# A three-block kernel on one core: float64 weights converted in the expert block and the last block, and the last block run as two passes over the tokens

## The chip, the cores and the metric

One core of a Trainium2 chip runs the program; the seven others are idle. The metric is the device time of one execution in microseconds, from the first to the last instruction with what lies around them; lower is better. The kernel before was timed three times: median 955.05 us, from 953.25 to 957.42.

## The reference

Three blocks follow each other. The second and third work on N = 4·576 = 2304 tokens of width 512.

```python
# 1 attention, B=4, H=8, S=576, D=64; bias is a small net of |i-j|, per head
scores = 0.125 * q @ k.T + bias[h]          # softmax over keys, then @ v
# 2 experts: E=8, each token goes to one expert, 512 -> 1024 -> 512
h  = np.maximum(x[mask] @ w1[e], 0.0);  out[mask] = gate * eom * (h @ w2[e])
# 3 last block, 512 -> 2048 -> 512; w_in and w_out are float64
h = x @ w_in;  g = h * np.cos(h);  out = g @ w_out
```

## The kernel before, in words

The program is one straight list of instructions, written in the order of the Python loops; every engine runs its own in that order and waits on semaphores. There are four stages.

**Bias table** (0 to 47.5 us): a table of biases is made and stored to DRAM.

**Attention** (47.5 to 305.7 us): 16 pairs of heads (`n`), each in five units `u` of two 128-row query tiles (the fifth has one). In a step, TensorE does the scores of unit `u` (L524, into two PSUM buffers `ps_s`), transposes the exponentials of the unit before (L560, into `Tp`), and does some of the products with V (L602; the table `AV_AT` says which of the ten products `(g, k)` stands how many steps after which unit). VectorE adds the bias and takes the row minimum (L534, which frees `ps_s`) and copies half of the transposes (L573); ScalarE does the exponentials (L545) and the other half (L571).

**Expert block** (`moe_dense`, 305.7 to 537.9 us): 64 steps of 24 matmuls, each float32 operand split into a high and a low part in the format fp32r, three products for one. L802 makes the low part of a weight tile on VectorE.

**Last block** (`moe2`, 537.9 us to the end): six groups of 384 tokens; for each, 16 chunks `f` of 128 hidden units; so 96 steps of 12 matmuls for the first layer (L1381, into `ph`) and 9 for the second (L1421, into three accumulators `py`), which runs four steps behind (`LAG3`). Between them the cosine: ScalarE L1316, VectorE L1321 to L1323, ScalarE L1395 and L1396, VectorE L1400, and then the split of `g` into `gh` (ScalarE L1406) and `gl` (GpSimd L1407). A group's sums leave through `o` (L1428 ScalarE, L1430 VectorE).

**The conversion.** `w_in` and `w_out` arrive as pairs of 32-bit words. The class `Doubles` cuts them into 64 pieces of 128 x 256 numbers. Each piece is loaded (L700, `raw`), turned into float32 by four VectorE instructions (L711 and L713 are a first `half()`, L716 and L718 a second) and an addition on GpSimd (L720), and stored to a DRAM tile `Wi` or `Wo` (L721), from where the last block's weights are loaded again (L792, `xc` or `Bp`), and split (L800, L802). `attention` converts 24 pieces: in each of pairs 1 to 12 a half after units 1 and 3 and two halves after unit 4 (`CV_AT`). `moe_dense` converts the other 40, as many halves in a step as a running cost on VectorE leaves room for (`STEP`, 3.2 us), the last ones behind its last step.

The order around the change is that of the Python calls. Two things in it matter. In attention, `softmax(n, u)` and, for `u` of 4, `convert(n, u)` follow each other, so that VectorE has the conversion ahead of the next pair's first L534. At the end of `moe_dense`, the remaining halves stand ahead of the last additions to `xT` (L1187) and of the last weight splits (L802), and the first tile `tk` of the last block (L1316) takes memory that the last of these splits reads.

Of the kernel before, what the change touches and what calls it, by code (L numbers as in the profile page):

```python
# [11 lines left out]
I32 = mybir.dt.int32  # L12
# [48 lines left out]
def build(tc, h, dbl, dbg=None):  # L61
    nc = tc.nc
    rw = dict(reuse_waits="tile")
    with ExitStack() as outer, ExitStack() as ctx:
# [17 lines left out]
            Wo=dpool.tile([DFF // 128, 128, DM], F32, name="Wo"),  # L82
        )
# [7 lines left out]
        with ExitStack() as low:  # L91
# [8 lines left out]
            attention(tc, h, ident, dram, xT, bpool, ps_t, gate, later, dense, cv)  # L100
# [17 lines left out]
        moe2(tc, h, dram, dense, later, wi, wo, magic)  # L118
# [283 lines left out]
def attention(tc, h, ident, dram, xT, bpool, ps_t, gate, later, dense, cv):  # L402
# [3 lines left out]
    with ExitStack() as ctx:  # L406
# [4 lines left out]
        cvp = low.enter_context(tc.tile_pool(name="p1d", bufs=2, side="right"))  # L411
# [66 lines left out]
        def after(G):  # L478
# [12 lines left out]
            if at == len(ROWS) - 1:  # L491
                load_v(1)
                gate.fetch()
                if cv:
                    cv.open(cvp, 24, 2, 3)
# [57 lines left out]
        def transposes(n, u):  # L553
# [8 lines left out]
            if u < 4:  # L562
# [52 lines left out]
        def convert(n, u):  # L615
            for _ in range(CV_AT[u] if cv and 0 < n < 13 else 0):
                cv.half()

# [4 lines left out]
        while t <= len(seq) or av:  # L623
            n, u = seq[t] if t < len(seq) else (None, None)
            if n is not None:
# [24 lines left out]
                if u == 4:  # L650
                    convert(n, u)
# [15 lines left out]
            if n is not None:  # L667
                if u < 4:
                    convert(n, u)
# [8 lines left out]
CV_AT = (0, 1, 0, 1, 2)  # L678
AV_AT = {1: ((0, 0, 1), (0, 1, 2), (0, 2, 2), (0, 3, 3)),
# [200 lines left out]
def moe_dense(tc, h, ident, dram, xT, dense, gate, later, cv):  # L880
    nc = tc.nc
    rw = dict(reuse_waits="tile")
    with ExitStack() as c2:
# [3 lines left out]
        if cv:  # L887
            cv.open(dpool, 40, 3, 2)
# [31 lines left out]
        for s in range(len(seq) + LAG2):  # L920
# [26 lines left out]
            if s in (NEXT_AT, NEXT_AT + 1):  # L947
                dense.load(B, s - NEXT_AT, 4, True)
# [18 lines left out]
X_AT, X2_AT, ADD_AT, GROUP_AT, HALF_AT, NEXT_AT = 21, 34, 48, 57, 60, 61  # L967
# [239 lines left out]
def doubles(tc, h, dram):  # L1207

    pieces = []
    for half in range(2):  # L1210
        for q in range(4 * half, 4 * half + 4):
            for c in range(NP_):
                pieces.append((h["w_in"].bitcast(I32)[128 * c:128 * c + 128, 512 * q:512 * q + 512], dram["Wi"][q, :, c, :]))
    for c in range(DFF // 128):
        for i in range(2):
            pieces.append((h["w_out"].bitcast(I32)[128 * c:128 * c + 128, 512 * i:512 * i + 512],
                           dram["Wo"][c, :, 256 * i:256 * i + 256]))
# [117 lines left out]
def moe2(tc, h, dram, dense, later, wi, wo, bias):  # L1335
# [4 lines left out]
    with ExitStack() as ctx:  # L1340
        pool = lambda name, bufs, **kw: ctx.enter_context(tc.tile_pool(name=name, bufs=bufs, reuse_waits="tile", **kw))
        xp, wp, gp, tp, op = (pool("p3x", 1), pool("p3w", 1), pool("p3g", 5), pool("p3t", 3), pool("p3o", 3))
        ps_h, ps_o = pool("ps_h", 5, space=PSUM), pool("ps_y", 1, space=PSUM)
        xg, xsp, d = {}, {0: dense.group}, {}
# [29 lines left out]
        def layer1(s):  # L1374
            g, f = divmod(s, FC)
# [35 lines left out]

        def layer2(s):
            g, f = divmod(s, FC)
            hi, lo = d[s]["hi"], d[s]["lo"]
            del d[s]
            if f == 0:
                acc[:] = [ps_o.tile([128, DM], F32, name=f"py{t}") for t in range(GT // 128)]
            for t in range(GT // 128):
                ts_ = slice(128 * t, 128 * t + 128)
                for n, (x, w) in enumerate(((hi, w_out[f][0]), (hi, w_out[f][1]), (lo, w_out[f][0]))):  # L1420
                    nc.tensor.matmul(acc[t], x[:, ts_], w, start=(f == 0 and n == 0), stop=(f == FC - 1 and n == 2))  # L1421
                if f == FC - 1:
                    o = op.tile([128, DM], F32, name="o")
                    out = h["out"][g * GT + 128 * t:g * GT + 128 * t + 128, :]
                    final = s == G * FC - 1 and t == GT // 128 - 1
                    near, far = (slice(0, DM // 2), slice(DM // 2, DM)) if final else (slice(0, DM),) * 2
                    if t % 2 == 0:
                        nc.scalar.activation(out=o[:, near], in_=acc[t][:, near], func=AF.Copy, scale=-2.0)  # L1428
                    if t % 2 or final:
                        nc.vector.tensor_scalar(out=o[:, far], in0=acc[t][:, far], scalar1=-2.0, scalar2=None,  # L1430
# [94 lines left out]
```

## Time and profile before

| | |
|---|---|
| three runs, median | 955.05 us |
| the profiled execution | 953.91 us, span 952.1 us, mean granted clock 0.987 |
| TensorE matmul busy | 917.5 us (96%) |
| VectorE busy | 651.8 us (68%) |
| ScalarE busy | 541.1 us (57%) |
| GpSimd busy | 303.5 us (32%) |

The profile is one execution; a line such as L524 is a line of the kernel before. Matmuls are pipelined and each row has its latency in it, so that TensorE counts as busy also where short bubbles lie between groups of matmuls. What a group really takes is the distance from its start to the next group's start. PE is TensorE, PEld its weight loads, DVE is VectorE, ACT ScalarE, POOL GpSimd, and SPq the queue of SyncE, which issues nearly all DMAs.

### The profile page before, as it was taken

The numbers are of one execution on the slowest core, as the hardware profiler recorded it, in microseconds if no ns is written. First come the engines' busy times: TensorE is split into PE (matmuls) and PEld (weight loads), VectorE is DVE, ScalarE is ACT, GpSimd is POOL, SyncE is SP. The second block draws the span as 40 slices with busy tenths as digits, with TensorE's granted clock in tenths as the row PEclk, the third lists the DMA queues.
The fourth block names the chain that finished last, engine by engine and source line by source line (L and its number), as shares of the span: only waits on it lengthen the run. The fifth ranks groups of instructions, "written<-read, shape, count | busy, mean of one in ns | idle before, by whom it ended". The sixth has DMA issues, their size and how long they took to land.

```text
span 952.1 us, 19180 instructions
## 1 busy us (share of the span) xinstructions
PE 917.5 (96%) x7145; PEld 779.4 (82%) x7146; DVE 651.8 (68%) x1472; ACT 541.1 (57%) x1153; POOL 303.5 (32%) x406
## 2 busy tenths in 40 slices
PE   7989999999999999999999989999999999999997
PEld 4666666666666899999899979999999999999995
DVE  8948888888867677788699898354444544544542
ACT  7967777777777434253263476455544554554542
POOL 0034554545555021213231225223233232232222
PEclk9979999999999999999999999999999999999999
DMA  7883536644537473537868531010100200100001
GB/s 215 275 293 111 170 123 218 199 146 139 183 115 243 155 244 135 181 100 232 276 224 277 193 115 52 1 67 1 50 17 1 67 1 1 67 1 1 34 1 36
DMA packets 62241, 118.04 MB, mean 124 GB/s; under 512 B 6664, under 2 KB 21532, under 8 KB 62140
## 3 DMA queue, kind: packets, MB, share of 16 engines
q1 hardware_dynamic: 61708, 116.45, 37.6%
q8 instruction: 58, 0.95, 0.4%
q14 instruction: 43, 0.35, 0.1%
q10 hardware_dynamic: 432, 0.29, 0.1%
HBM read 83.11 MB, written 33.60 MB: 123 GB/s over the span
## 4 chain that ended last, share of the span: by engine, by line
PE 69%; DVE 5%; DMA 2%; ACT 2%; issue 1%; POOL 0%; SPq 0%; DVEq 0%; POOLq 0%; ACTq 0%
PE py L1421 21%; PE ph L1381 20%; PE pl L854 9%; PE po L872 8%; PE pa L602 3%; PE ps_s L524 3%; PE Tp L560 2%; DMA Wo<-f32a 1%; DVE f32a L713 1%; ACT e L545 1%; DVE w1l L802 1%; DVE f32a L711 1%; DVE s L534 1%; DMA Fd<-lp 1%; DVE xl L826 0%
## 5 line engine op out<-in xcount | busy, mean ns | idle before, releaser
L1407 POOL TENSOR_TENSOR gl<-tg,gh 128x384 fp32r<-128x384 f32 x96 | 97.8, 1020 | 277.3 <-ACT gh L1406 163.6
L1316 ACT ACTIVATE tk<-ph,magic 128x384 f32<-128x384 f32 x96 | 55.5, 580 | 165.8 <-PE ph L1381 165.8
L1321 DVE TENSOR_SCALAR tk<-tk 128x384 f32<-128x384 f32 x96 | 36.6, 381 | 156.5 <-ACT tk L1316 156.5
L1381 PE MATMUL ph<-xh,w0l 128*128 128x384 f32 x384 | 129.5, 337 | 0.0
L1381 PE MATMUL ph<-xl,w0h 128*128 128x384 f32 x384 | 129.2, 336 | 0.0
L1381 PE MATMUL ph<-xh,w0h 128*128 128x384 f32 x384 | 129.2, 336 | 0.0
L1421 PE MATMUL py<-w1h,gh 128*128 128x512 f32 x288 | 113.7, 395 | 4.1 <-ACT gh L1406 4.1
L545 ACT ACTIVATE e<-s,mn 128x576 f32<-128x576 f32 x144 | 110.2, 767 | 6.5 <-DVE mn L534 6.3
L1421 PE MATMUL py<-w1h,gl 128*128 128x512 f32 x288 | 113.8, 395 | 0.0
L1421 PE MATMUL py<-w1l,gh 128*128 128x512 f32 x288 | 113.3, 393 | 0.0
L720 POOL TENSOR_TENSOR f32a<-f32a,raw 128x256 f32<-128x256 f32 x64 | 49.2, 769 | 195.9 <-DVE raw L718 174.0
L534 DVE CUSTOM_DVE_ANT_0 s<-ps_s,Bp 128x576 f32<-128x576 f32 x112 | 81.0, 755 | 40.8 <-PE ps_s L524 32.4
L524 PEld LDWEIGHTS ps_s<-HL 64*128 64x128 f32 x768 | 58.1, 191 | 38.6 <-DVE mn L534 20.0
L524 PE MATMUL ps_s<-HL 64*128 64x288 f32 x768 | 77.5, 319 | 10.3 <-DVE mn L534 8.8
L857 ACT ACTIVATE hh<-pl 128x288 fp32r<-128x288 f32 x64 | 26.3, 410 | 101.1 <-PE pl L854 98.0
L854 PE MATMUL pl<-xh,w0h 128*128 128x288 f32 x256 | 78.3, 306 | 1.8 <-DVE hl L858 1.8
L602 PE MATMUL pa<-eT,V 128*64 128x320 f32 (+1 forms) x512 | 79.4, 420 | 0.0
L854 PE MATMUL pl<-xl,w0h 128*128 128x288 f32 x256 | 76.4, 299 | 2.4 <-DVE xl L826 2.4
L854 PE MATMUL pl<-xh,w0l 128*128 128x288 f32 x256 | 75.5, 295 | 0.0
L872 PE MATMUL po<-hh,w1h 128*128 128x288 f32 x256 | 75.5, 295 | 0.0
L872 PE MATMUL po<-hl,w1h 128*128 128x288 f32 x256 | 75.5, 295 | 0.0
L872 PE MATMUL po<-hh,w1l 128*128 128x288 f32 x256 | 75.4, 295 | 0.0
(226 smaller groups left out, 2222.1 us busy)
## 6 DMA issues: line engine op xcount, KB each, us to landing
Bp<-in_w SPq DMA_DIRECT2D x38, 512.0 KB, 5.3
Bd<-ev SPq DMA_DIRECT2D x36, 295.5 KB, 4.7
Rqk<-in_qk SPq DMA_DIRECT2D x16, 576.0 KB, 5.6
raw<-in_w_in SPq DMA_DIRECT2D x32, 256.0 KB, 4.4
raw<-in_w_out SPq DMA_DIRECT2D x32, 256.0 KB, 3.8
Bp<-Bd SPq DMA_DIRECT2D x28, 288.0 KB, 5.1
X<-xT SPq DMA_DIRECT2D x7, 1152.0 KB, 5.6
V<-in_v SPq DMA_DIRECT2D x16, 320.0 KB, 4.2
```

Of the source, the lines that this page charges most:

```text
L524: nc.tensor.matmul(p[:, hf, :HF], w, y, start=(x == 0), stop=(x == 2))
L534: nc.vector.tensor_tensor_reduce(out=h2(s), in0=ps[:, :, :HF], in1=h2(bias(hp, i)), scale=-0.125, scalar=3e38, op0=ALU.add, op1=ALU.min, a ...
L545: nc.scalar.activation(out=e[:, par, :], in_=s, func=AF.Exp, bias=mn, scale=-1.0, accum_out=acc)
L602: nc.tensor.matmul(pa[64 * par:64 * par + 64, :W], d["V"][:, k, par, :], x, start=(k == 0), stop=(k == 4))
L720: self.tc.nc.gpsimd.tensor_tensor(out=af[:], in0=af[:], in1=low, op=ALU.add)
L854: nc.tensor.matmul(ps[:, :HF], w[:, c, :], x[:, c, :], start=(n == 0), stop=(n == len(terms) - 1))
L872: nc.tensor.matmul(self.acc[d][:, :HF], w[:, ds_], x, start=(f == 0 and n == 0), stop=(f == self.FC - 1 and n == 2))
L1316: nc.scalar.activation(out=k, in_=hh, func=AF.Identity, scale=INV2PI, bias=magic)
L1321: nc.vector.tensor_scalar(out=k, in0=k, scalar1=-MAGIC, scalar2=None, op0=ALU.add)
L1381: nc.tensor.matmul(ps[:, :GT], w[:, c, :], x[:, c, :], start=(n == 0), stop=(n == 3 * NP_ - 1))
L1407: nc.gpsimd.tensor_tensor(out=lo, in0=g, in1=hi.bitcast(F32), op=ALU.subtract)
L1421: nc.tensor.matmul(acc[t], x[:, ts_], w, start=(f == 0 and n == 0), stop=(f == FC - 1 and n == 2))
```

## The change

Conversion leaves attention altogether. The expert block converts 32 pieces (the first halves of `w_in` and of `w_out`), the last block the other 32, one or two halves in a step from its second step on. So that the second half of the weights is wanted later, the last block runs over the tokens twice: groups 0 to 5 with hidden chunks 0 to 7, whose sums are stored to a DRAM tile `Y1`, and then groups 5 to 0 with chunks 8 to 15, which add them back. Tokens of five groups are loaded and split a second time. Loads of the late weights stand at steps 13, 24, 34 and 45 (`LATE_AT`). In attention the products with V move: of the four of the first query half that came one, two, two and three steps after their unit, two now come at two steps and two at three; and the second copy of unit 3's transposes moves from ScalarE to VectorE. A constructor argument (`dynamic_dma_scratch_size=1024`) makes room in SBUF.

```diff
@@ attention
-            if at == len(ROWS) - 1:  ...  cv.open(cvp, 24, 2, 3)
-                    if qh == 0 or u == 3:
+                    if qh == 0:
                         nc.scalar.activation(out=dst, in_=Tp[qh], func=AF.Copy)
-                if u == 4:
-                    convert(n, u)
...
-CV_AT = (0, 1, 0, 1, 2)
-AV_AT = {1: ((0, 0, 1), (0, 1, 2), (0, 2, 2), (0, 3, 3)),
+AV_AT = {1: ((0, 0, 2), (0, 1, 2), (0, 2, 3), (0, 3, 3)),
@@ moe_dense
-            cv.open(dpool, 40, 3, 2)
+            cv.open(dpool, 32, 3, 2)
-            if s in (NEXT_AT, NEXT_AT + 1):
-                dense.load(B, s - NEXT_AT, 4, True)
@@ doubles: first half of w_in, first half of w_out, then quarter by quarter
+    for which in range(2):
+        for q in range(4):
+            part(which, q)
+    for q in range(4, 8):
+        for which in range(2):
+            part(which, q)
@@ moe2
+        HC = FC // 2
+        units = [(g, 0) for g in range(G)] + [(g % G, 1) for g in range(G - 1, 2 * G - 1)]
+        at = lambda s: (*units[s // HC], s % HC)
...
-                if f == FC - 1:
+                if j == HC - 1:
                     o = op.tile([128, DM], F32, name="o")
...
+                    if half == 0:
+                        if t % 2 == 0:
+                            nc.scalar.activation(out=o, in_=acc[t], func=AF.Copy, scale=-2.0)
+                        else:
+                            nc.vector.tensor_scalar(out=o, in0=acc[t], scalar1=-2.0, scalar2=None, op0=ALU.mult)
+                        nc.sync.dma_start(out=dram["Y1"][rows(g, t), :], in_=o)
+                        continue
+                    final = s == len(units) * HC - 1 and t == GT // 128 - 1
+                    for c in (slice(0, DM // 2), slice(DM // 2, DM)) if final else (slice(0, DM),):
+                        nc.vector.scalar_tensor_tensor(out=o[:, c], in0=acc[t][:, c], scalar=-2.0, in1=y1[t][:, c],
+                                                       op0=ALU.mult, op1=ALU.add)
...
+        if cv:
+            cv.open(cp, 32, 3, 2)
+        for q, when in zip(range(4, 8), LATE_AT):
...
+            if cv and s:
+                for _ in range(1 + s % 2):
+                    cv.half()
...
+                if nx != g:
+                    if j == 0:
+                        load_x(nx)
...
+                if half and j == 2:
+                    load_y(g)
+LATE_AT = (13, 24, 34, 45)
```

VectorE in attention, from the last L534 of unit 3 to the first of the next pair (`s` and `mn` are the biased scores and their minimum, `eT` the transposes' copy). Before:

```order
L534 ISA s,mn<-ps_s,Bq 128x576
L534 ISA mn 128x1
L573 COPY eT_930<-Tp 128x2x4x64
L716 TENSOR_SCALAR raw_1633<-f32a 128x256
L718 SCALAR_TENSOR_TENSOR raw_1633<-raw_1633 128x256
L534 ISA s,mn<-ps_s,Bq 128x576
L534 ISA mn 128x1
L711 TENSOR_SCALAR f32a<-raw_1656 128x256
L713 SCALAR_TENSOR_TENSOR f32a<-raw_1656,f32a 128x256
L716 TENSOR_SCALAR raw_1656<-f32a 128x256
L718 SCALAR_TENSOR_TENSOR raw_1656<-raw_1656 128x256
L534 ISA s,mn<-ps_s,Bp 128x576
```

Now (L532 is the former L534, L571 the former L573):

```order
L532 ISA s,mn<-ps_s,Bq 128x576
L532 ISA mn 128x1
L571 COPY eT_924<-Tp 128x2x4x64
L532 ISA s,mn<-ps_s,Bq 128x576
L532 ISA mn 128x1
L571 COPY eT_924<-Tp 128x2x4x64
L532 ISA s,mn<-ps_s,Bp 128x576
```

Six conversion instructions are gone from ahead of the last two L534 there, and one copy has come.

TensorE in the same place, from the scores of unit 3 to those of the next pair's second unit. Before:

```order
L524 MATMUL ps_s<-HL 128x288 x12
L560 MATMUL Tp<-ident,e 128x64 x16
L602 MATMUL pa_927<-eT_929,V 64x256 x2
L524 MATMUL ps_s<-HL,QR_126 128x288 x6
L560 MATMUL Tp<-ident,e 128x64 x16
L602 MATMUL pa_927<-eT_929,V 64x256 x4
L592 MATMUL Tp<-ident,et 128x128 x4
L524 MATMUL ps_s<-HL 128x288 x12
L560 MATMUL Tp<-ident,e 128x64 x10
L602 MATMUL pa_927<-eT_929,V 64x256 x2
L524 MATMUL ps_s<-HL 128x288 x12
```

Now:

```order
L522 MATMUL ps_s<-HL 128x288 x12
L558 MATMUL Tp<-ident,e 128x64 x16
L522 MATMUL ps_s<-HL,QR_126 128x288 x6
L558 MATMUL Tp<-ident,e 128x64 x16
L600 MATMUL pa_921<-eT_923,V 64x256 x4
L590 MATMUL Tp<-ident,et 128x128 x4
L522 MATMUL ps_s<-HL 128x288 x12
L558 MATMUL Tp<-ident,e 128x64 x10
L600 MATMUL pa_921<-eT_923,V 64x256 x4
L522 MATMUL ps_s<-HL 128x288 x12
```

Two matmuls with V have gone from unit 3's step to the next pair's first step.

VectorE at the turn from the expert block to the last block (L1187 adds to `xT`, L802 is a weight's low part, L711 to L718 the conversion, L1321 to L1323 the reduction of the first angles). Before:

```order
L711 TENSOR_SCALAR f32a<-raw_8302 128x256
L713 SCALAR_TENSOR_TENSOR f32a<-raw_8302,f32a 128x256
L716 TENSOR_SCALAR raw_8302<-f32a 128x256
L718 SCALAR_TENSOR_TENSOR raw_8302<-raw_8302 128x256
L1187 SCALAR_TENSOR_TENSOR xT<-xb,ohb,xT 128x288 x2
L1187 SCALAR_TENSOR_TENSOR xT<-xa,ohb,xT 128x288 x2
L802 TENSOR_TENSOR w1l_5432<-Bp,w1h_5431 128x1024
L802 TENSOR_TENSOR w1l_5434<-Bp,w1h_5433 128x1024
L1321 TENSOR_SCALAR tk<-tk 128x384
L1322 SCALAR_TENSOR_TENSOR tr<-tk,ph 128x384
L1323 SCALAR_TENSOR_TENSOR tr<-tk,tr 128x384
```

Now (L1175 is the former L1187, L792 the former L802, L701 to L708 the conversion, L1318 to L1320 the reduction):

```order
L1175 SCALAR_TENSOR_TENSOR xT<-xb,ohb,xT 128x288 x2
L1175 SCALAR_TENSOR_TENSOR xT<-xa,ohb,xT 128x288 x2
L792 TENSOR_TENSOR w1l_5213<-Bp,w1h_5212 128x1024
L792 TENSOR_TENSOR w1l_5215<-Bp,w1h_5214 128x1024
L1318 TENSOR_SCALAR tk<-tk 128x384
L1319 SCALAR_TENSOR_TENSOR tr<-tk,ph 128x384
L1320 SCALAR_TENSOR_TENSOR tr<-tk,tr 128x384
L701 TENSOR_SCALAR f32a<-raw_8190 128x256
L703 SCALAR_TENSOR_TENSOR f32a<-raw_8190,f32a 128x256
L706 TENSOR_SCALAR raw_8190<-f32a 128x256
L708 SCALAR_TENSOR_TENSOR raw_8190<-raw_8190 128x256
```

The last two of the conversion's pieces stood ahead of the additions to `xT` before (one is shown); now none does, and a whole piece follows the first reduction.

## Rows read from the trace of the kernel before

**Rows 1.** Busy time by stretch: turn to the last block, last block; us, engines, PEclk, DMA.
```profile
537.90:556.50 18.60, 14.49 (x73) 13.07 (x72) 16.33 (x29) 11.39 (x20) 3.67 (x5) 0.91 0.19 59
556.50:944.70 388.20, 388.20 (x1948) 351.63 (x1946) 203.55 (x384) 199.22 (x408) 118.61 (x115) 1.00 0.09 29
```
**Rows 2.** Chain that ended last, in order of time: start us, us, what.
```profile
552.74 3.90 PE py L1421 x9
...
650.76 2.10 PE py L1421 x9
```
**Rows 3.** Page part 5, groups: busy us, mean ns, then idle before and releaser.
```profile
L1421 PE MATMUL py<-w1h,gh 128*128 128x512 f32 x288 | 113.7, 395 | 4.1 <-ACT gh L1406 4.1
...
L720 POOL TENSOR_TENSOR f32a<-f32a,raw 128x256 f32<-128x256 f32 x64 | 49.2, 769 | 195.9 <-DVE raw L718 174.0
...
L854 PE MATMUL pl<-xh,w0h 128*128 128x288 f32 x256 | 78.3, 306 | 1.8 <-DVE hl L858 1.8
```
**Rows 4.** Timeline of VectorE at the turn to the last block.
```profile
537.67 0.85 DVE L711 TENSOR_SCALAR f32a<-raw 128x256 int32<-128x256 int32 x1
...
541.97 1.43 DVE L1187 SCALAR_TENSOR_TENSOR xT<-xb,ohb,xT 128x288 f32<-128x288 f32 x2
...
544.18 2.35 DVE L802 TENSOR_TENSOR w1l<-Bp,w1h 128x1024 fp32r<-128x1024 f32 x2
```
**Rows 5.** Timeline of ScalarE at the turn to the last block.
```profile
546.62 1.06 ACT L1316 ACTIVATE tk<-ph,magic 128x384 f32<-128x384 f32 x2 [5.51 <-PE ph L1381]
...
552.18 0.51 ACT L1406 ACTIVATE gh<-tg 128x384 fp32r<-128x384 f32 x1
```
**Rows 6.** Timeline of TensorE, 171 to 176 us: a pair's turn with a conversion.
```profile
172.35 1.07 PE L524 MATMUL ps_s<-HL 64*128 64x288 f32 x12
...
175.34 0.94 PE L524 MATMUL ps_s<-HL 64*128 64x288 f32 x10 [0.28 <-DVE mn L534]
```
**Rows 7.** Timeline of VectorE in the same stretch, 171 to 176 us.
```profile
171.11 1.08 DVE L711 TENSOR_SCALAR f32a<-raw 128x256 int32<-128x256 int32 x1
...
173.85 0.75 DVE L534 CUSTOM_DVE_ANT_0 s<-ps_s,Bp 128x576 f32<-128x576 f32 x1
```
**Rows 8.** Timeline of TensorE, 66.6 to 70 us: a turn with no conversion.
```profile
66.70 1.05 PE L524 MATMUL ps_s<-HL 64*128 64x288 f32 x12
...
69.40 0.80 PE L524 MATMUL ps_s<-HL 64*128 64x288 f32 x8 [0.28 <-DVE mn L534]
```
**Rows 9.** Tile `raw`: instructions, duration ns min/median/max; last, its loads' time to landing.
```profile
L711 DVE TENSOR_SCALAR f32a<-raw x64: 279/287/1397, 72.4 to 540.2; 128x256 int32<-128x256 int32 x64
L713 DVE SCALAR_TENSOR_TENSOR f32a<-raw,f32a x64: 424/427/932, 72.8 to 540.8; 128x256 int32<-128x256 int32 x64
L716 DVE TENSOR_SCALAR raw<-f32a x64: 275/295/1387, 79.0 to 541.3; 128x256 int32<-128x256 int32 x64
L718 DVE SCALAR_TENSOR_TENSOR raw<-raw x64: 425/427/849, 79.3 to 541.6; 128x256 f32<-128x256 uint32 x64
...
DMA to landing us min/median/max: 2.7/3.9/6.7
```
**Rows 10.** Line L1323: duration ns min/median/max.
```profile
L1323 DVE SCALAR_TENSOR_TENSOR tr<-tk,tr x96: 557/558/1420, 548.2 to 936.4; 128x384 f32<-128x384 f32 x96
```
**Rows 11.** VectorE by line, 560 to 944 us: busy us, mean ns.
```profile
L1323 DVE SCALAR_TENSOR_TENSOR tr<-tk,tr 128x384 f32<-128x384 f32 x92 | 57.5, 625 | 3.2
...
L1322 DVE SCALAR_TENSOR_TENSOR tr<-tk,ph 128x384 f32<-128x384 f32 x91 | 50.5, 554 | 3.2
L1321 DVE TENSOR_SCALAR tk<-tk 128x384 f32<-128x384 f32 x91 | 34.8, 382 | 155.2 <-ACT tk L1316 155.2
```
**Rows 12.** Timeline of VectorE at the end of the program.
```profile
944.34 0.69 DVE L1430 TENSOR_SCALAR o<-py 128x512 f32<-128x512 f32 x1 [5.59 <-PE py L1421]
```
**Rows 13.** GpSimd by line, 560 to 944 us.
```profile
L1407 POOL TENSOR_TENSOR gl<-tg,gh 128x384 fp32r<-128x384 f32 x94 | 95.8, 1020 | 265.5 <-ACT gh L1406 151.8 <-PE py L1421 113.7
L1372 POOL TENSOR_TENSOR xl<-xg,xh 128x384 fp32r<-128x384 f32 x20 | 23.1, 1157 | 0.0
```

More of the change, by code (lines that the diff above doesn't have):

```diff
@@ L99, in build @@
             cv = doubles(tc, h, dram) if dbl else None
[L100 removed]
+            attention(tc, h, ident, dram, xT, bpool, ps_t, gate, later, dense)
             if dbg == "attn":
@@ L399, in bias_table, with attention @@
         evac(ROWS[-1])
-def attention(tc, h, ident, dram, xT, bpool, ps_t, gate, later, dense, cv):
+def attention(tc, h, ident, dram, xT, bpool, ps_t, gate, later, dense):
     nc = tc.nc
@@ L1209, in doubles, with part @@
     pieces = []
-    for half in range(2):
-        for q in range(4 * half, 4 * half + 4):
+    def part(which, i):
+        if which == 0:
             for c in range(NP_):
[L1213 to L1217, printed above, removed]
+                pieces.append((h["w_in"].bitcast(I32)[128 * c:128 * c + 128, 512 * i:512 * i + 512], dram["Wi"][i, :, c, :]))
+        else:
+            for c in (2 * i, 2 * i + 1):
+                for k in range(2):
+                    pieces.append((h["w_out"].bitcast(I32)[128 * c:128 * c + 128, 512 * k:512 * k + 512],
+                                   dram["Wo"][c, :, 256 * k:256 * k + 256]))
+    for which in range(2):
[4 more added lines that the diff above has]
+            part(which, q)
     return Doubles(tc, pieces, 256)
@@ L1410, in moe2, with rows, load_y @@
         acc = []
+        def rows(g, t):
+            return slice(g * GT + 128 * t, g * GT + 128 * t + 128)
+        def load_y(g):
+            for t in range(GT // 128):
+                y1[t] = yp.tile([128, DM], F32, name="y1")
+                nc.sync.dma_start(out=y1[t], in_=dram["Y1"][rows(g, t), :])
         def layer2(s):
-            g, f = divmod(s, FC)
+            g, half, j = at(s)
+            f = HC * half + j
             hi, lo = d[s]["hi"], d[s]["lo"]
             del d[s]
-            if f == 0:
+            if j == 0:
                 acc[:] = [ps_o.tile([128, DM], F32, name=f"py{t}") for t in range(GT // 128)]
@@ L1420, in layer2 @@
                 for n, (x, w) in enumerate(((hi, w_out[f][0]), (hi, w_out[f][1]), (lo, w_out[f][0]))):
[L1421 to L1422 removed]
+                    nc.tensor.matmul(acc[t], x[:, ts_], w, start=(j == 0 and n == 0), stop=(j == HC - 1 and n == 2))
+                if j == HC - 1:
                     o = op.tile([128, DM], F32, name="o")
[L1424 to L1430, printed above, removed]
[L1431 to L1434 removed]
@@ L1436, in moe2 @@
+                    for c in (slice(0, DM // 2), slice(DM // 2, DM)) if final else (slice(0, DM),):
+                        nc.vector.scalar_tensor_tensor(out=o[:, c], in0=acc[t][:, c], scalar=-2.0, in1=y1[t][:, c],
+                                                       op0=ALU.mult, op1=ALU.add)
+                        eng = nc.scalar if final and c.start == 0 else nc.sync
+                        eng.dma_start(out=h["out"][rows(g, t), c], in_=o[:, c])
         warm = op.tile([1, 1], F32, name="o")
@@ L1437, in moe2 @@
         nc.scalar.activation(out=warm, in_=bias[0:1, :], func=AF.Sin, scale=0.0)
-        for i, q in enumerate(range(4, 8)):
+        if cv:
+            cv.open(cp, 32, 3, 2)
+        for q, when in zip(range(4, 8), LATE_AT):
             for j in range(2):
-                if i:
-                    later.add([(3 * i + 1 + j, lambda q=q, j=j: dense.load(B, j, q, True))])
-                later.add([(3 * i + 3 + j + k, lambda q=q, j=j, k=k: split_w(q, j, k)) for k in range(2)])
-        N = G * FC
+                later.add([(when + j, lambda q=q, j=j: dense.load(B, j, q, True))])
+                later.add([(when + 2 + 2 * j + k, lambda q=q, j=j, k=k: split_w(q, j, k)) for k in range(2)])
```

46 lines of the change are left out of this document (21 added, 25 removed).

## The prediction

> **What bounds the kernel now.** I read the stretches first, then the chain of waits, then the timelines of the two places where the change takes VectorE work away. In the last block TensorE is busy 388.20 of 388.20 us at full clock, VectorE 203.55 [rows 1]; the chain there is TensorE alone, 2.10 us for nine matmuls of the second layer [rows 2]. The 1948 records of that stretch, 21 to a step, are 92.8 steps, so 4.18 us a step. This stage can't gain; it can only lose if another engine needs more than 4.18 us a step.
>
> In the expert block the VectorE groups that TensorE waits for cost little: 1.8 us over the block before the first layer's matmuls [rows 3]. Eight pieces less there are worth nothing that I can see.
>
> The turn between the two costs more. The first matmuls of the second layer wait 4.1 us for `gh` [rows 3], and then nine of them take 3.90 us instead of 2.10 [rows 2], since the granted clock of that stretch is 0.91 [rows 1]: after the idle time TensorE works for a while at the lower of its two levels, 1.2 instead of 2.4 GHz. Together 4.1 + 1.8 = 5.9 us. What ends last there is VectorE: two whole pieces run from 537.67 to 541.97, then the additions, then two splits from 544.18 to 546.53 [rows 4], and ScalarE's first L1316 starts at 546.62, right behind them, and `gh` at 552.18 [rows 5]. ScalarE's wait is put down to TensorE, whose `ph` had long been ready; the memory that the splits read is what it needs.
>
> In attention TensorE has hardly a pause, and yet one place shows VectorE. At a turn of pairs the scores of the next pair start at 172.35 and the bulk of those of its second unit at 175.34, 2.99 us later, waiting for the row minimum at the end [rows 6]. Ahead of that minimum VectorE has a piece: from 171.11, L711 at 1.08 us, so that L534 starts at 173.85 [rows 7]. At the one turn without a conversion the same two starts are 66.70 and 69.40, 2.70 us apart [rows 8].
>
> **The change, part by part.** *Attention.* Only the turns carry conversions that TensorE waits for: 2.99 - 2.70 = 0.29 us each. `CV_AT` puts two halves behind unit 4 in 12 pairs, so 12 x 0.29 = 3.5 us. The halves after units 1 and 3 lie beside V products. Bounds: nothing (the turn is set by something else after all) to 12 x (0.29 + 0.28), when the wait of 0.28 that is left at a turn without conversion [rows 8] went too: 6.8 us. I take 3.5, the row that is nearest. The V products are the same in number. Two go from unit 3's step to the turn's first step, where TensorE waits for the minimum anyway, so they are hidden there; if that cover is gone they only stand where they would have stood. In unit 3's step TensorE then gets ahead to the transposes of unit 3, which need the same exponentials as before. I take 0. The copy moved to VectorE comes after unit 4's minimum and ahead of the next pair's, in the room that the conversion leaves: 0.
>
> *Turn to the last block.* The two pieces ahead of the additions go, so these, the splits and the first L1316 come up to 541.97 - 537.67 = 4.3 us sooner, at about 542.4. But one whole piece now stands behind the first reduction and a half ahead of the first L1400, alone 0.29 + 0.43 + 0.30 + 0.43 = 1.44 us and 0.71 [rows 9]. Its load is new: it is issued by SP behind the last store of `xT`, which waits for the additions, and takes 3.9 us to land [rows 9]; additions done at about 540.3, two issues, so landed near 545.2, a microsecond after VectorE is ready for it. VectorE waits in order, and behind the waiting L711 stand the next reduction and the first L1400, for which `gh` and TensorE wait. Running through the chain, reduction done 544.4, piece 545.2 to 546.6, second reduction 548.1, half 548.8, L1400 and `gh` 549.9; TensorE has its first-layer steps ahead done at about 552.74 - 4.1 = 548.6 [rows 2, 3]. So it waits about 1.5 to 2 us instead of 4.1, and I put the low clock behind a shorter pause at 0.7 instead of 1.8. That is 5.9 - 2.4 = 3.5 us. Bounds: 1.9 us when the load is two microseconds later than that, 5.9 when nothing is left.
>
> *Last block, first 43 steps.* Per unit of eight steps TensorE needs 8 x 4.18 = 33.4 us. VectorE alone: 8 x (0.38 + 0.55 + 0.56 + 0.55), with L1400 taken as long as L1322 [rows 10, 11], is 16.3; six pieces 8.6; one and a half splits at 2.35 / 2 [rows 4] 1.8; one accumulator 0.69 [rows 12]; sum 27.4. That fits. But it does not stay alone: L1323 takes 558 ns free and up to 1420 [rows 10], L711 287 and up to 1397, L713 427 and up to 932 [rows 9], and in [rows 7] the L711 of 1.08 us ran while GpSimd worked. GpSimd will have, per unit, 8 x 1.02 + 4 x 1.16 [rows 13] + 6 x 0.77 [rows 3] = 17.4 us, 52% of the time, where it has 31% now [rows 1]. The worst of every such instruction would add 8 x 0.86 + 6 x (1.11 + 0.50 + 1.09 + 0.42) = 25.6 and make 53 of 33.4. What L1323 pays now is a mean of 625 [rows 11], (625 - 558) / (1420 - 558) = 8% of its worst, a quarter of GpSimd's share; so at 52% between 13% (30.7, fits) and 52% (40.7, too much). Before VectorE is late for TensorE it may lose about a step, 4 us, since the second layer runs four steps behind, and at each change of group it waits for the accumulators and starts level again. I take 13% and put the loss at 1 us; bounds 0 and the price of the rivals below.
>
> *The rest.* Twelve accumulator sets instead of six leave while TensorE does a first-layer group, 2.1 us against 0.69: 0. Loads and stores of `Y1` and the second load of the tokens stand five or more steps ahead of their use: 0. At the very end VectorE adds what ScalarE shared: one more half of 0.69, 0.4 us.
>
> Sum: -3.5 - 3.5 + 1 + 0.4 = -5.6. The profiled execution took 953.91, so 948.3; the median of the runs is 1.1 above it: **949.4 us**.
>
> **The rivals.**
> *Two engines take turns.* If no VectorE instruction with both operands in SBUF, nor a conversion, ran while GpSimd does, the last block would be set by their sum: 8 x (0.38 + 0.56) + 8.6 + 1.8 = 17.9 for VectorE and 17.4 for GpSimd, 35.3 per unit against 33.4. That is 1.9 x 43 / 8 = 10.2 us, and -3.5 - 3.5 + 10.2 + 0.4 = +3.6: 958.7. For it speak the 1.08 us of L711; against it that L713's worst, 932, is about twice its 427 and not more.
> The Trainium skill, page "SBUF — State Buffer", section "Who interferes with whom", says that VectorE and GpSimd share one pair of ports under an exclusive lock, the loser waiting for the whole instruction. By that rule this rival is the forecast; the trace has L711 as the rule wants it, and L713 rather slowed than stopped.
>
> *VectorE sets the last block.* Slower than before: with 40% of the worst, 10.2, VectorE needs 37.6 per unit, 4.2 too much, x 43 / 8 = 22.6 us, and the sum is +16: 971. It decides from about 4.8 + 6.6 = 11.4 us on, 2.1 per unit, which is 32% of the worst. Against it: now a quarter of GpSimd's share, not all of it.
>
> *The load is late.* If the turn keeps 4 of its 5.9 us, the gain there is 1.9: 951.0.
>
> *Attention doesn't move.* If unit 4's step is bound by the exponentials, and the minimum only follows, the 3.5 fall away: 952.9. For it: TensorE shows few pauses; against it the turn without conversion.
>
> **How the numbers follow.** Half a per cent, 4.8 us, is what a measurement of this kernel can tell from no change: faster is below 950.3, slower above 959.8. Chances: forecast 0.50 (its own range 945 to 953), taking turns 0.16, VectorE sets the block 0.11, late load 0.12, attention still 0.11. Faster: three quarters of the forecast, a third of the late load and some of the others, 0.46. Slower: all of VectorE's rival and a fifth of the turns', 0.14. The rest 0.40. The range leaves out VectorE's rival and a little below: 944 to 960.
>
> **What would show it.** Turns in attention 2.7 us apart with no conversion ahead of the minimum; TensorE's first second-layer matmul waiting 2 us or less, near 546.5 in the new span (all is 3.5 us earlier by then); 4.18 us a step in the first 43 steps, with VectorE below 32 us per unit. Wrong it is if the chain in the first half of the last block has VectorE lines in it, or steps longer than 4.2 us.

## The result: 0.8% slower, because TensorE waits at the changes of group in the first pass

The changed kernel took 962.75 us (median of 4 runs, 961.72 to 965.35) against 955.26 for the kernel before (4 runs, 953.25 to 957.42); the ratio is 1.0078, 95% interval 1.0061 to 1.0094. 949.4 was predicted, with a range of 944 to 960. Its profiled execution has a span of 960.5 us where the one before had 952.1. By the starts of the first matmuls of each stage the 8.4 us divide as follows; "turn" is the first five steps of the last block.

| stretch | before | after | difference | predicted |
|---|---|---|---|---|
| attention | 258.18 | 254.70 | -3.5 | -3.5 |
| expert block | 232.35 | 232.51 | +0.2 | 0 |
| turn | 18.43 | 13.93 | -4.5 | -3.5 |
| rest of the last block, to the last matmul | 388.51 | 404.06 | +15.6 | +1 |
| end | 7.1 | 7.9 | +0.8 | +0.4 |

Attention came as forecast, the turn and the end within a microsecond; the last block is off by 14.6 us. (L1383 is the former L1381, L1432 the former L1421, L1373 the low part of the tokens, formerly L1372, L1318 to L1320 the former L1321 to L1323, L1402 the former L1400, L1439 the former L1430, L701 to L710 the conversion.)

### The profile page after: what moved, and what is told of

Read it like the earlier page. It is cut to its first block, busy times and chain, and to the rows that moved or that the text cites. A ratio compares the mean times of both kernels' runs of the same rounds, so it can differ in the third digit from the quotient of the medians.

```text
span 960.5 us, 19323 instructions
## 1 busy us (share of the span) xinstructions
PE 914.0 (95%) x7145; PEld 779.0 (81%) x7146; DVE 695.5 (72%) x1506; ACT 549.5 (57%) x1157; POOL 330.0 (34%) x426
## 4 chain that ended last, share of the span: by engine, by line
PE 60%; DVE 11%; issue 3%; DMA 3%; POOL 1%; ACT 1%; SPq 1%; DVEq 0%; POOLq 0%; ACTq 0%
PE py L1432 17%; PE ph L1383 15%; PE pl L844 9%; PE po L862 9%; PE pa L600 3%; PE ps_s L522 3%; DVE f32a L701 1%; PE Tp L558 1%; DVE tr L1319 1%; DVE tr L1320 1%; DVE f32a L703 1%; DMA Wo<-f32a 1%; DVE tk L1318 1%; DVE tg L1402 1%; DVE raw L706 1%
## 5 line engine op out<-in xcount | busy, mean ns | idle before, releaser
L1409 POOL TENSOR_TENSOR gl<-tg,gh 128x384 fp32r<-128x384 f32 x96 | 102.1, 1064 | 190.8 <-ACT gh L1408 109.0
L1383 PE MATMUL ph<-xl,w0h 128*128 128x384 f32 x384 | 130.2, 339 | 9.9 <-POOL xl L1373 9.9
L532 DVE CUSTOM_DVE_ANT_0 s<-ps_s,Bp 128x576 f32<-128x576 f32 x112 | 81.1, 756 | 69.9 <-PE ps_s L522 57.3
L1383 PE MATMUL ph<-xh,w0h 128*128 128x384 f32 x384 | 130.0, 339 | 0.0
L1383 PE MATMUL ph<-xh,w0l 128*128 128x384 f32 x384 | 129.9, 338 | 0.0
L710 POOL TENSOR_TENSOR f32a<-f32a,raw 128x256 f32<-128x256 f32 x64 | 48.0, 749 | 237.0 <-DVE raw L708 206.5
L1432 PE MATMUL py<-w1h,gl 128*128 128x512 f32 x288 | 114.3, 397 | 0.5 <-POOL gl L1409 0.5
L1432 PE MATMUL py<-w1h,gh 128*128 128x512 f32 x288 | 114.0, 396 | 0.5 <-ACT gh L1408 0.5
L1432 PE MATMUL py<-w1l,gh 128*128 128x512 f32 x288 | 113.9, 396 | 0.0
L1318 DVE TENSOR_SCALAR tk<-tk 128x384 f32<-128x384 f32 x96 | 45.1, 470 | 75.9 <-ACT tk L1313 75.9
L1383 PEld LDWEIGHTS ph<-xl,w0h 128*128 128x128 f32 x384 | 72.3, 188 | 15.3 <-POOL xl L1373 11.5
L522 PEld LDWEIGHTS ps_s<-HL 64*128 64x128 f32 x768 | 56.0, 185 | 32.8 <-DVE mn L532 13.0
L522 PE MATMUL ps_s<-HL 64*128 64x288 f32 x768 | 74.7, 312 | 5.8 <-DVE mn L532 4.4
L1383 PEld LDWEIGHTS ph<-xh,w0h 128*128 128x128 f32 x384 | 72.5, 189 | 4.0
```

The costliest lines, as they stand in the source:

```text
L522: nc.tensor.matmul(p[:, hf, :HF], w, y, start=(x == 0), stop=(x == 2))
L532: nc.vector.tensor_tensor_reduce(out=h2(s), in0=ps[:, :, :HF], in1=h2(bias(hp, i)), scale=-0.125, scalar=3e38, op0=ALU.add, op1=ALU.min, a ...
L710: self.tc.nc.gpsimd.tensor_tensor(out=af[:], in0=af[:], in1=low, op=ALU.add)
L1318: nc.vector.tensor_scalar(out=k, in0=k, scalar1=-MAGIC, scalar2=None, op0=ALU.add)
L1383: nc.tensor.matmul(ps[:, :GT], w[:, c, :], x[:, c, :], start=(n == 0), stop=(n == 3 * NP_ - 1))
L1409: nc.gpsimd.tensor_tensor(out=lo, in0=g, in1=hi.bitcast(F32), op=ALU.subtract)
```

## The profile after

The stretches of the last block, columns as in [rows 1]: the turn, the first pass, the second pass.

```profile
534.40:548.50 14.10, 13.22 (x72) 12.16 (x71) 12.38 (x26) 9.53 (x17) 2.41 (x3) 1.00 0.58 184
548.50:728.00 179.50, 169.40 (x823) 150.33 (x822) 165.94 (x291) 98.30 (x192) 89.03 (x91) 0.98 0.38 118
728.00:952.30 224.30, 224.30 (x1127) 204.08 (x1125) 128.11 (x234) 116.99 (x241) 79.00 (x75) 1.00 0.21 68
```

The second pass is as full as all of the block was before. In the first TensorE is idle for 10 of 179.5 us, the granted clock is 0.98, and VectorE (third engine column) is busy 92% of it. Part 5 of the page, the groups that answer to [rows 3]:

```profile
L1383 PE MATMUL ph<-xl,w0h 128*128 128x384 f32 x384 | 130.2, 339 | 9.9 <-POOL xl L1373 9.9
L710 POOL TENSOR_TENSOR f32a<-f32a,raw 128x256 f32<-128x256 f32 x64 | 48.0, 749 | 237.0 <-DVE raw L708 206.5
L1432 PE MATMUL py<-w1h,gh 128*128 128x512 f32 x288 | 114.0, 396 | 0.5 <-ACT gh L1408 0.5
```

The 4.1 us for `gh` are now 0.5; instead 9.9 us of waits stand before the first layer, for the low parts of the tokens. TensorE's timeline has all five of them, one at each change of group in the first pass:

```profile
566.63 0.44 PE L1383 MATMUL ph<-xl,w0h 128*128 128x384 f32 x1 [2.85 <-POOL xl L1373]
603.83 0.44 PE L1383 MATMUL ph<-xl,w0h 128*128 128x384 f32 x1 [1.75 <-POOL xl L1373]
638.35 0.44 PE L1383 MATMUL ph<-xl,w0h 128*128 128x384 f32 x1 [0.60 <-POOL xl L1373]
673.98 0.44 PE L1383 MATMUL ph<-xl,w0h 128*128 128x384 f32 x1 [1.71 <-POOL xl L1373]
710.87 0.44 PE L1383 MATMUL ph<-xl,w0h 128*128 128x384 f32 x1 [2.98 <-POOL xl L1373]
```

The five steps that hold them took 8.24, 6.23, 5.07, 6.18 and 9.01 us, against 4.18 for a free one: 13.8 of the 15.6 us. The other group changes, in the second pass, where nothing is converted, show no wait. The chain of waits at the first of them (start us, us, what; "..." stands for rows left out, here and below):

```profile
561.38 0.47 DVE tg L1402
561.84 0.28 DVE tk L1318
...
562.14 0.57 DVE tr L1319
...
562.73 1.17 DVE tr L1320
563.91 0.21 DVE raw L706
...
564.15 0.44 DVE raw L708
...
564.70 0.04 POOL f32a L710
564.74 0.65 issue
565.39 1.19 POOL xl L1373
566.59 0.04 issue
566.63 0.61 PE ph L1383 x2
567.24 3.05 PE py L1432 x9
570.30 2.68 PE ph L1383 x12
572.97 2.10 PE py L1432 x9
```

Read it backwards. The matmul at 566.63 needs the last low part, L1373. GpSimd works in order, and in the last step of a unit L1373 stands behind the conversion's addition L710, which needs L708 on VectorE, which is late. And after the pause nine matmuls take 3.05 us, not 2.10, at a granted clock of 0.63: part of them at the lower of the two levels. After the last wait, of 2.98 us, nine take 3.64; after the waits of 1.75 and 1.71 us they take 2.09.

In attention, TensorE's scores at a turn of pairs, to be laid beside [rows 6]:

```profile
169.28 1.07 PE L522 MATMUL ps_s<-HL 64*128 64x288 f32 x12
171.61 1.43 PE L522 MATMUL ps_s<-HL 64*128 64x288 f32 x12
```

The second row joins two things that [rows 6] has apart. Its first matmul comes 2.33 us after the first unit's, as before (2.31). The second one needs VectorE's row minimum; VectorE's row for it, and TensorE's row when the stretch is read from 172.02 us on:

```profile
171.84 0.08 DVE L532 DVE_READ_ACCUMULATOR2_ANT mn<- 128x1 f32 x1
171.98 0.94 PE L522 MATMUL ps_s<-HL 64*128 64x288 f32 x10
```

So the bulk of the second unit's scores comes 2.70 us after the first's, where it came after 2.99 in [rows 6]. It still follows the minimum.

## The experiments

Two theories stood at the start. *Order*: VectorE has just about enough time, and what costs is that something TensorE needs within a step stands in a queue behind the conversion. *Capacity*: VectorE needs more than TensorE's 33.4 us per unit of eight steps (the sum of its instructions' times is 35.8), so the wait can only change its place.

### The token split one step earlier

```diff
-                    if 3 <= j < 7:
-                        split_x(nx, j - 3)
-                    if 4 <= j < 8:
-                        lower_x(nx, j - 4)
+                    if 2 <= j < 6:
+                        split_x(nx, j - 2)
+                    if 3 <= j < 7:
+                        lower_x(nx, j - 3)
```

> The high and low parts of the next group's tokens (L1369 on ScalarE, L1373 on GpSimd) each stand one step earlier: at steps 2 to 5 and 3 to 6 of a unit of eight, not 3 to 6 and 4 to 7. Order theory: TensorE waits 10.7 us at the five changes of group only because the last L1373 stands behind the conversion's addition L710 in GpSimd's last step; a step more of room takes the wait and the low clock behind it away, 950 to 952 us, and the first matmul of a group no longer waits for L1373. Capacity theory: VectorE is busy 180.6 of 183 us between 545 and 728 us, so the steps cannot come closer whatever the order on GpSimd: at least 960 us, and the waits move from L1373 to the second layer's L1432 (gl, gh).

956.24 us (10 runs, 952.71 to 958.81), ratio to the kernel before 1.0006 [0.9992, 1.0021]: as fast as the kernel before, and 4 us above what the order theory expected. Part 5 of its page:

```profile
L1383 PE MATMUL ph<-xl,w0h 128*128 128x384 f32 x384 | 129.6, 338 | 0.0
L1432 PE MATMUL py<-w1h,gh 128*128 128x512 f32 x288 | 113.7, 395 | 6.6 <-DVE o L1439 3.9
```

The wait for L1373 is gone entirely, and the rest of the last block fell from 404.06 to 394.90 us. Neither theory had it whole: a new wait of 3.9 us in four places has come, for VectorE's copy of the second sum, L1439, which frees the accumulator for the next group. The other 2.73 us of the 6.6 are at the turn, which took 16.14 us, not 13.93 (below).

### The two passes without their conversion

The changed kernel with `attention` converting 24 pieces and the expert block 40, as before (`CV_AT` and `cv.open` restored, `cv.half` out of `moe2`). Attention keeps the change's new table and copy.

> The last block runs in two passes as in the changed kernel, but all 64 pieces are converted where the kernel before converted them (24 in attention, 40 in the expert block). Both theories: the stalls at the changes of group are gone, since GpSimd has no L710 there and VectorE no conversion (35.8 - 9 us of 33.4 per unit); from the traces +3.5 in attention, +4.5 at the turn, -15.6 in the last block: 962.75 - 7.6 = 955 us. A third theory, that the two passes cost something by themselves (second split of the tokens, evictions to Y1 and back, load_y): 958 us or more, with waits at the changes of group that stay.

966.39 us, ratio 1.0113 [1.0097, 1.013]: the last block is as expected and the sum is not. The rest of the last block took 389.04 us against 388.51 with one pass, and no step had a wait. So the second pass itself (second split of the tokens, sums out and in) costs half a microsecond at most (in two kernels below whose last block is that of the kernel before, the same stretch took 389.1 and 389.2), and the conversion in it the other 15. But attention took 267.23 us, 9.1 more than before; the last two experiments find out why.

### One instruction of each step from VectorE to ScalarE

```diff
-    nc.vector.tensor_scalar(out=k, in0=k, scalar1=-MAGIC, scalar2=None, op0=ALU.add)
+            nc.scalar.activation(out=k, in_=k, func=AF.Identity, bias=unmagic)
```

> The subtraction of the rounding constant (L1318 of the changed kernel, 0.555 us of VectorE in each step) is done by ScalarE instead, as an Identity with a bias; all else as in the changed kernel, the order on GpSimd too. Capacity theory: VectorE's need per unit of eight steps falls from 35.8 by 8 x 0.555 = 4.4 to 31.4 us, under TensorE's 33.4: the waits for L1373 go, 950 to 952 us. Order theory: the last L1373 still stands behind L710 and its operands; the wait at a change of group shrinks but stays at about 1 us each, 955 to 958 us.

959.45 us, ratio 1.0048 [1.0031, 1.0065]: more than either theory expected. VectorE's busy time between 545 and 728 us fell from 169.30 to 159.75, and the waits hardly (L1385 and L1375 are L1383 and L1373 of the changed kernel):

```profile
L1385 PE MATMUL ph<-xl,w0h 128*128 128x384 f32 x384 | 130.0, 339 | 8.3 <-POOL xl L1375 8.3
```

A VectorE with time to spare still leaves 8.3 of 9.9 us. This falls outside the capacity theory: what binds the last low part is its place. By the code, L710 of step 7 follows that step's halves, these follow the reduction of step 6, which needs step 6's matmuls; from there only about a step is left until TensorE wants the next group.

### The split ahead of the halves within its step

The block with `split_x` and `lower_x` moved ahead of `cv.half()`, at the same steps.

> Within a step the token split (L1369, L1373) is issued ahead of the conversion's halves, so that on GpSimd the step's L1373 stands ahead of that step's L710 instead of behind it; the steps themselves are as in the changed kernel. Order theory: the last L1373 no longer waits for L710's operands from VectorE (0.74 us of L710 itself and up to 1.2 us of its wait): 2 us of each stall go, 952 to 955 us. Capacity theory: VectorE sets the pace, at least 959 us, and TensorE waits for gl or gh instead.

959.52 us, ratio 1.0039 [1.0023, 1.0055]; the waits for L1373 are 5.6 us, those for L1439 1.7. The time is the one that the capacity theory expected; the waits are not, which it had at `gl` or `gh`. The rest of the last block took 398.80 us, a little over half of the gain of a whole step's room, by the code because a low part still stands behind the addition of the step before.

### ScalarE copies the sums of the first pass

With the split one step earlier, and all three sums of the first pass through `nc.scalar.activation`.

> With the token split one step earlier (956.24 us), TensorE's wait for L1373 was gone, and four waits of 1.45, 1.18, 0.41 and 0.86 us for VectorE's copy of the second sum (o<-py1, L1439) had come, which with the low clock and gaps behind them make 5.1 us. Here ScalarE copies all three sums of the first pass. Order theory (a late VectorE costs time only where an instruction that TensorE needs within a step stands behind the conversion): these four waits go, 950 to 952 us. Capacity theory (VectorE has more work than the steps have time, 35.8 for 33.4 us): the wait comes back elsewhere, at gl or gh (L1432), and the time stays within 1.5 us of 956.

955.25 us, ratio 0.9995 [0.9979, 1.0012]. The waits for L1439 are gone, the rest of the last block is 390.74 us (394.90 with them), and no step of the first pass behind the turn is over 4.8 us. They did not come back elsewhere, as the capacity theory had it. (The low clock that the expectation names had no part in them: the granted clock of that stretch, 552.75 to 735 us in the kernel with the split one step earlier, was 1.00.) The time did not fall as the order theory had it either: the turn took 16.20 us.

### The halves behind the second layer

With the split one step earlier:

```diff
-            if cv and s:
-                for _ in range(1 + s % 2):
-                    cv.half()
             if 0 <= s - LAG3 < N:
                 layer2(s - LAG3)
+            if cv and s:
+                for _ in range(1 + s % 2):
+                    cv.half()
```

> With the token split one step earlier, and the halves of the conversion issued behind the second layer of their step instead of ahead of it, so that VectorE has the copy of a group's second sum (L1439) ahead of that step's one or two halves (2.1 us each pair); no work is taken from VectorE. Order theory: the four waits for L1439 go or shrink below 0.3 us each, 951 to 953 us. Capacity theory: VectorE's work is the same, 956 us, with waits for gl or gh instead.

954.47 us, ratio 0.9988 [0.997, 1.0006]. The rest of the last block is 389.98 us with VectorE's work unchanged: the waits for L1439 were order too. Over 24 steps of the first pass, columns as in [rows 1]:

```profile
605.00:706.00 101.00, 101.00 (x505) 90.86 (x504) 97.25 (x173) 59.53 (x117) 52.80 (x54) 1.00 0.43 138
```

VectorE is busy 96% of the stretch, more than in the changed kernel, and TensorE has no pause in it. That VectorE is nearly full is thus not what costs the time.

Here the turn took 18.08 us. Its ScalarE, in the timeline, shows why:

```profile
544.16 0.53 ACT L1397 ACTIVATE tr<-tr 128x384 f32<-128x384 f32 x1 [0.85 <-DVE tr L1320]
549.94 0.52 ACT L1369 ACTIVATE xh<-xg 128x384 fp32r<-128x384 f32 x1 [4.70 <-DMA xg<-X]
```

At step 2 the first tokens have not landed; their load was issued at 543.26, behind the last store of `xT`, and takes 6.7 us. ScalarE stands in order, so the next angles wait 4.70 us behind the split. In the kernel as changed the split stood a step later and this wait was 0.35 us. So the step that saved 9.2 us in the block cost 2 to 4 at its start, a granted clock of 0.50 from 552.80 to 556.20 us included.

### Attention's order as before

With the split one step earlier, and `AV_AT` and the copy of the kernel before.

> With the token split one step earlier (956.24 us), and attention's table of V products and its copies of the transposes as in the kernel before (fourth unit's second copy on ScalarE), still without conversion in attention. Attention took 258.2 us in the kernel before, 254.7 to 255.9 in the changed one, and 267.2 with the new table and copies but with the conversion in it. If the departure of the conversion alone gives the gain: 255 us for attention, 956 us. If the new table and copies are what turns the free VectorE time into time: attention 258 us or more, 959 us. If they cost something even so: attention 252 to 254 us, 954 us.

955.92 us, ratio 1.001 [0.999, 1.0029]; attention 253.62 us. Inconclusive by itself; the pair of kernels below settles it. Its last block is that of the first experiment and took 17.91 us for the turn and 393.49 for the rest, where that took 16.14 and 394.90: so far apart two profiles of one block can lie.

### Without GpSimd's addition

> The changed kernel, with the conversion's addition on GpSimd (L710) left out for the 32 pieces of the last block, so that the low words of these weights are missing from the output; VectorE does all that it did. Order theory: the last L1373 no longer stands behind L710, which takes 0.74 us and waits up to 1.2 us for VectorE, so the waits at the changes of group fall below 1 us, some 954 us. Contention theory (VectorE's instructions are stretched by GpSimd's: L1320 0.824 us on the mean against 0.554 alone): with a quarter of GpSimd's work gone the mean of L1320 falls to about 0.75 and VectorE's busy time of 180.6 us by 5; both theories expect a gain, the means of the instructions tell how much of VectorE's lateness GpSimd makes.

952.47 us, ratio 0.9977 [0.9962, 0.9993]; the waits for L1373 are 3.7 us. So the addition, by its place in GpSimd's queue, was most of the wait (two of the three that are left are above the 1 us expected). The other question has a clear answer. VectorE by line, 561 to 704 us (busy us, mean ns), of the changed kernel:

```profile
L1320 DVE SCALAR_TENSOR_TENSOR tr<-tk,tr 128x384 f32<-128x384 f32 x32 | 26.0, 814 | 1.1
L1318 DVE TENSOR_SCALAR tk<-tk 128x384 f32<-128x384 f32 x32 | 18.2, 569 | 4.3 <-ACT tk L1313 4.3
L703 DVE SCALAR_TENSOR_TENSOR f32a<-raw,f32a 128x256 int32<-128x256 int32 x24 | 16.9, 706 | 0.8
```

and without the addition:

```profile
L1321 DVE SCALAR_TENSOR_TENSOR tr<-tk,tr 128x384 f32<-128x384 f32 x33 | 37.5, 1137 | 1.1
L703 DVE SCALAR_TENSOR_TENSOR f32a<-raw,f32a 128x256 int32<-128x256 int32 x26 | 11.1, 426 | 0.9
L1319 DVE TENSOR_SCALAR tk<-tk 128x384 f32<-128x384 f32 x33 | 11.7, 354 | 0.7 <-ACT tk L1314 0.7
```

L703 and the subtraction now run at their free durations, and the second reduction, expected at 750 ns, rose to 1137. All VectorE lines of the stretch together are 143.4 us for 32 steps and 148.1 for 33: 4.5 a step in both. The collisions moved and did not become fewer, so the contention theory's expectation failed.

### The order mended, with either attention

```diff
+                    for c in ((), (), (), (0,), (1,), (2, 3), (), ())[j]:
+                        split_x(nx, c)
+                    for c in ((), (), (), (), (0,), (1,), (2, 3), ())[j]:
+                        lower_x(nx, c)
```

in place of the four lines of the split, and the halves behind the second layer; the first kernel has attention's order of before, the second the new one.

> Only the order is mended; VectorE and GpSimd keep all their work in the last block. The token split: high parts at steps 3, 4, 5, 5 of a unit, low parts at 4, 5, 6, 6, so that ScalarE no longer stands waiting at step 2 for the first load of the tokens (4.70 us in the kernel with the halves behind the second layer, whose first five steps took 18.08 us and not 13.9) and no low part stands in the last step. The halves stand behind the second layer. In attention the table and the copies are those of the kernel before. Order theory: attention 253.6, turn 13.8, rest of the last block 390, in all 946 us of span, 948 us. Capacity theory, as far as it still stands: with the turn no longer late VectorE has no slack in the steps after it, and the waits come back, 953 us or more.

> The same order in the last block, but attention with the new table and copies. If these cost 1 to 2 us, as one profile against seven others said (253.62 us against 254.6 to 255.9): 949.5 us, 1.5 above the kernel with the order of before in attention; if that was chance: the same time as that kernel.

951.73 us, ratio 0.996 [0.9945, 0.9974], and 951.04 us, ratio 0.9951 [0.9935, 0.9967] (6 runs each). Both beat both kernels, and they don't differ: attention took 254.80 and 255.34 us, so the 253.62 above was chance. Part 5 of the second one's page:

```profile
L1383 PE MATMUL ph<-xl,w0h 128*128 128x384 f32 x384 | 129.4, 337 | 0.0
L1432 PE MATMUL py<-w1h,gl 128*128 128x512 f32 x288 | 113.8, 395 | 1.3 <-POOL gl L1409 1.3
L1432 PE MATMUL py<-w1h,gh 128*128 128x512 f32 x288 | 113.2, 393 | 0.5 <-ACT gh L1408 0.5
```

The turn took 13.59 us and the rest of the block 392.17. Of the 15.6 us all but 3.7 are back, without an instruction less. The expected 948 was not reached: with a prompt turn seven steps of the first pass take 4.30 to 5.41 us, with waits of 0.17 to 0.36 us for `gl` and `gh`. That much is left of the capacity theory: VectorE fits, with nothing to spare.

### Each edit of attention beside the conversion

The kernel before with `if qh == 0:` in place of `if qh == 0 or u == 3:`, and the kernel before with the first line of `AV_AT` alone.

> The kernel before, conversion in attention included, with one edit: the second copy of the fourth unit's transposes on VectorE. With both edits of attention beside the conversion, attention took 267.2 us and not 258.2. If the copy makes it, because VectorE is the busy engine there and gets one instruction more of about 0.75 us in each of 16 pairs: attention 264 to 268 us, 962 us. If the table makes it: 258 us and 955 us.

> The kernel before, conversion in attention included, with the other edit alone: two of the products with V one step later each. If the table makes the 9 us: attention 264 to 268 us, 962 us; if the copy makes them: 257 to 259 us, 955 us.

968.08 us with the copy, ratio 1.0133 [1.0111, 1.0155]; 954.94 with the table, ratio 0.9995 [0.9981, 1.0008]. Attention took 267.94 and 258.46 us. VectorE (six rows) and TensorE (the last) at a turn of pairs, with the copy:

```profile
192.25 1.09 DVE L711 TENSOR_SCALAR f32a<-raw 128x256 int32<-128x256 int32 x1
193.38 0.84 DVE L713 SCALAR_TENSOR_TENSOR f32a<-raw,f32a 128x256 int32<-128x256 int32 x1
194.33 0.29 DVE L716 TENSOR_SCALAR raw<-f32a 128x256 int32<-128x256 int32 x1
194.66 0.43 DVE L718 SCALAR_TENSOR_TENSOR raw<-raw 128x256 f32<-128x256 uint32 x1
195.00 0.68 DVE L573 COPY eT<-Tp 128x512 f32<-128x512 f32 x1
195.60 0.75 DVE L534 CUSTOM_DVE_ANT_0 s<-ps_s,Bp 128x576 f32<-128x576 f32 x1
...
195.83 0.53 PE L560 MATMUL Tp<-ident,e 64*128 64x64 f32 x10 [1.27 <-DVE eT L573]
```

The copy of 0.68 us stands behind a whole piece, and TensorE's next transposes wait 1.27 us for it. Without the conversion the same copy costs nothing. The kernel with the copy is 6 us slower than expected: in its profile the expert block, which has no edit, took 236.56 us too, 4.2 more than in the kernel before. Its first 12 us ran at a granted clock of 0.72, for 0.86 before; whether that comes from the copy stays open.

## Why the prediction was wrong

*Attention, -3.5: right in mechanism; that the sum agrees so well is partly luck.* The 2.99 us at a turn became the 2.70 forecast, and a pair takes 0.3 us less (from one unit's scores to the same unit's a pair later, 160.29 to 175.11 us in the changed kernel, 14.82 us; before, 166.60 to 181.75, 15.15). But that holds for eight pairs, the fourth to the eleventh, and gives 2.4 us. The first pair, which never had a conversion, was 1.5 us shorter (with the order of before and no conversion it took 18.03 and 19.19 us in two profiles, so most of that is chance), the thirteenth 0.9, and 1.3 were lost behind it. The prediction priced the copy and the table at nothing, and beside no conversion both are: the two mended kernels say so. That the copy would have cost 9.8 us beside the conversion the profile before did not show.

*Turn, -3.5: right in mechanism, 1 us too small.* `gh` was awaited for 0.54 us, not the 1.5 to 2 worked out, and no low clock followed.

```profile
545.70 0.51 PE L1432 MATMUL py<-w1h,gh 128*128 128x512 f32 x1 [0.54 <-ACT gh L1408]
```

*Last block, +1: wrong*, measured +15.6. Two sentences failed. The first is "Before VectorE is late for TensorE it may lose about a step, 4 us, since the second layer runs four steps behind". That is so for `gh` and `gl` and was applied to everything. The low parts of the next group's tokens have no such lag: the last of them stands in the step before its use, behind L710. The second is "Loads and stores of `Y1` and the second load of the tokens stand five or more steps ahead of their use: 0": the loads do, but their split, which comes after, stands one step ahead. It entered the sum only as GpSimd time (4 x 1.16), and its place was priced nowhere. Moving the split a step took 9.2 us off. A third term at nothing, "Twelve accumulator sets instead of six leave while TensorE does a first-layer group", failed behind it: with the split mended, four waits of 3.9 us for the accumulators came out, and freeing them earlier took another 4 to 5 off.

The 13% of the worst collisions was too small a share as well: L1320's mean of 814 ns is (814 - 558) / (1420 - 558) = 30%. But VectorE at that level did not set the time; with the order mended it was as busy, and TensorE lost 1.5 to 4.5 us of the 15.6. The rival "VectorE sets the last block" put 22.6 us on that block (971 in all) and "two engines take turns" 10.2 (958.7); the measured 15.6 and 962.75 lie between the two, and neither names the cause. The 35.3 us per unit of the second would be 4.4 us a step, while most steps of the mended kernels took 4.21.

What that rival starts from is nevertheless so, and more strictly than the prediction read it, which had L713 (now L703) "rather slowed than stopped". GpSimd and VectorE in the changed kernel:

```profile
560.03 1.06 POOL L1373 TENSOR_TENSOR xl<-xg,xh 128x384 fp32r<-128x384 f32 x1
560.25 1.12 DVE L703 SCALAR_TENSOR_TENSOR f32a<-raw,f32a 128x256 int32<-128x256 int32 x1
...
564.70 0.74 POOL L710 TENSOR_TENSOR f32a<-f32a,raw 128x256 f32<-128x256 f32 x1 [1.21 <-DVE raw L708]
564.81 0.91 DVE L703 SCALAR_TENSOR_TENSOR f32a<-raw,f32a 128x256 int32<-128x256 int32 x1
```

Both times L703 ends 0.28 us after GpSimd's instruction has ended, though the one took 1.12 us and the other 0.91; so do all 25 L703 of this kernel that started beside GpSimd. L701 ends 0.15 us behind it, L1320 0.41. So they are stopped until GpSimd is done; what they still need then is less than their free duration (0.43 us for L703), and this is one reason why the two engines together need less than the sum of 35.3 us. How much of the difference it makes was not worked out. L1319 and L1402, which read `ph` from PSUM, are not held up: 555 and 545 ns, beside GpSimd or not. The Trainium skill's exclusive lock ("SBUF — State Buffer", "Who interferes with whom") agrees here with L701 and with L703.

"The load is late" did not happen: VectorE waited 0.61 us for the first piece. The load that came late, in the experiments that moved the split to step 2, was another, that of the tokens.

The prediction's own test named the sign that came: VectorE lines in the chain of the last block's first half, and steps longer than 4.2 us, five of them from 5 to 9 (a free step of the first pass takes 4.21, also where nothing is converted).

## What to carry to other kernels

When work is added to an engine that works in order, slack is to be counted for each consumer by itself: list what stands behind the new instructions in every queue they pass through (here VectorE, then GpSimd through the addition), and for each how many steps later TensorE reads it. An operand that is read once per group can have less room than one that is read in every step. And where a queue must wait for a load, an edit that brings the reader forward is only as early as the load.

## What the runs showed that was not expected

- Taking a quarter of GpSimd's work away did not make VectorE's instructions shorter on the sum: 4.5 us a step before and after, with the second reduction at 1137 ns for 814 and L703 at 426 for 706.
- VectorE's summed durations can exceed the time that passes without holding TensorE up: 104.9 us of instructions in the 101.00 us of the kernel with the halves behind the second layer, of which they cover 97.25. In the timelines one instruction starts before the one ahead of it has ended, as 195.00 + 0.68 and the L534 at 195.60. So the 35.8 us per unit that the capacity theory rests on say too much.
- One copy of 0.68 us in a pair cost 9.8 us over attention beside the conversion and nothing without it.
- A VectorE instruction that starts beside GpSimd's and works on SBUF alone waits for the end of GpSimd's instruction and then takes a fixed rest: 0.15 us for L701, 0.28 for L703, 0.41 for L1320.
